# A fused retention and token-mixing kernel on one Trainium2 core: 64-row transposes, a transposed product for wq, other queues and a new order

## The chip, the cores and the metric

The kernel runs on one core of a Trainium2 chip. The core has a matrix engine (TensorE, PE in the profile, with its weight loads as PEld), three engines for elementwise work (VectorE or DVE, ScalarE or ACT, GpSimd or POOL), a queue engine that issues the transfers (SyncE or SP), and 16 DMA engines. Each engine works through its own instructions in the order of the program and waits for the others by semaphores. TensorE writes to PSUM, which has eight banks; VectorE and ScalarE read it, GpSimd does not.

The metric is the time of one execution on the device in microseconds. Lower is better.

## The reference, cut to what matters

```
# q, k, v: [4, 8, 768, 64] f32; w_q, w_k: [512, 64]; w_out: [512, 512]
gamma[h] = 1 - 2 ** (-5 - h)
for t in range(768):
    state = gamma * state + k[t] v[t]^T          # per batch and head, 64 x 64
    y[t]  = q[t] state / sqrt(64)
x  = y, heads side by side                       # [4, 768, 512]
wq = x @ w_q                                     # [4, 768, 64]
wk = x @ w_k
mixed = (wq wk^T / sqrt(64)) @ x                 # over the tokens of a batch
out   = relu(mixed) @ w_out                      # [4, 768, 512] f32
```

## The kernel before

The 768 tokens of a batch are cut into three pairs of chunks of 128 tokens; with four batches there are 12 pairs, numbered 0 to 11. The first half of the work on a pair is the retention in chunked form. The decay is put into v (factors `fv`) and into the result (factors `fy`), so that within a chunk the result is a masked product of scores with v, and between chunks a running state of 64 x 64 for each head is kept in PSUM bank 7. The second half is the mixer: wq and wk of the pair, then, once for each batch, z = wk^T x (`zm`), then for each pair mixed^T = z^T wq^T (`mx`), relu and the product with w_out (`pj`).

Nothing is scheduled by a compiler. A list of tokens, `ORDER`, is written out by hand and run through once; each token emits the instructions of one step. A token reads `name.pair.part:engine@bank`. `ck`, `cq` and `cv` cast the loaded k, q and v to bf16 (v with its factors); `trk` and `trq` transpose k and q on TensorE into PSUM, `ekT` and `eqT` copy them out; `sc` makes the scores of half the heads, `eat` masks them on VectorE; `st` adds to the state, `es` copies it out; `ia` and `in` are the products within a chunk and with the state; `ex` writes x. `xt` and `exT` transpose x; `wqk` makes wq and wk in one product; `ewq` copies wq out (twice side by side), `ew` copies wk; `tw` transposes wq and `ewt` copies it; `zm`, `ez`, `mx`, `r`, `pj` and `eo` follow. `W` and `WO` cast the weights. `fill` emits matmuls on zeros, whose results nobody reads.

A transpose of 128 rows by 128 columns is one TensorE instruction with a weight load; a pair has 8 each in `trk` (L344), `trq` (L359) and `xt` (L483), and 2 in `tw` (L523). The scores (L379) and the products with the state (L419) have 64 rows, and their two halves of heads lie in the upper and the lower 64 rows of the array and in different banks. The other line numbers that the text uses: L137 is a copy or cast on ScalarE, L138 one on VectorE or GpSimd, L292 the fills, L316 `cv`, L391 `eat`, L433 `st`, L453 `ia`, L467 `ex`, L497 `wqk`, L545 `zm`, L565 `mx`, L587 `pj`, L616 the stores, L156 the loads.

All transfers but the first go through the SP queue, in the order of a second list:

```
LOADS = """
q0 v0 k1 q1 v1 k2 q2 v2 k3 q3 v3 w k4 q4 v4 k5 q5 v5 o k6 q6 v6 k7 q7 v7 k8 q8 v8 k9 q9 v9 k10
q10 s0 v10 k11 s1 q11 s2 v11 s4 s3 s5 s6 s7 s8 s10 s11/0 s11/1 s9
""".split()
```

`k3` is the load of k of pair 3 (512 KB in pieces of 512 bytes), `w` and `o` are the weights, `s4` is the store of pair 4, and `s11/0` that of half a pair. There are 18 staging slots for k, q and v; a load waits until the cast of the load 18 places before it is done, and a store until both halves of its pair are copied out. The weights have staging of their own. Ten buffers hold results that wait for their store.

Of the kernel before, what the change touches and what calls it, by code (L numbers as in the profile page):

```python
# [9 lines left out]
FP32 = mybir.dt.float32  # L10
# [6 lines left out]
ck.0.1:V cq.0.0:A ck.0.0:P fill.20@6 trk.0@6 cq.0.1:V trq.0@0 cv.0.0:V ekT.0:A eqT.0:A st.0.0  # L17
ck.1.1:V ck.1.0:A cv.0.1:P sc.0.0@0 eat.0.0:V es.0.0:A sc.0.1@2 eat.0.1:V fill.1@6 trk.1@6
cq.1:A fill.3@0 trq.1@0 st.0.1 cv.1.0:P ia.0.1@2 ekT.1:A ck.2.0:A in.0.1@2 eqT.1:V ia.0.0@2
sc.1.0@0 es.0.1:A sc.1.1@4 cq.2:A ck.2.1:P st.1.0 ex.0:V trk.2@6 cv.1.1:P trq.2@2 eat.1.1:V  # L20
es.1.0:A eat.1.0:V eqT.2:A ekT.2:V ck.3.1:A ck.3.0:A xt.0@4 st.1.1 sc.2.0@2 cv.2.0:P cq.3:A
sc.2.1@0 exT.0:V es.1.1:V cv.2.1:P ia.1.0@4 cv.3.0:P in.1.0@4 eat.2.0:V in.1.1@4 ia.1.1@4
cv.3.1:P ck.4.1:P ex.1:V st.2.0 in.2.0@2 fill.1@6 trk.3@6 es.2.0:A cv.4.0:P cv.4.1:P fill.1@4
trq.3@4 ekT.3:A eat.2.1:V W:A ia.2.0@2 eqT.3:V ia.2.1@2 in.2.1@2 xt.1@6 sc.3.0@4 ex.2:V st.3.0
wqk.0@0 xt.2@1 exT.1:A wqk.1@6 es.3.0:A sc.3.1@2 eat.3.0:V ewq.0:A in.3.1@4 exT.2:V st.3.1
wqk.2@1 ew.0:A cq.4:A ia.3.0@4 eat.3.1:V ewq.1:A ewq.2:V ew.2:V ia.3.1@4 tw.1@2 ex.3:V cv.5.0:P
ew.1:A ck.4.0:A trq.4@6 trk.4@3 tw.0@1 ewt.1:V tw.2@0 es.3.1:A ck.5.1:A ekT.4:V eqT.4:V ck.5.0:A
ewt.2:A xt.3@4 st.4.0 cq.5:A fill.2@2 sc.4.0@2 trk.5@6 ewt.0:A exT.3:V ekT.5:V zm.0@4 trq.5@5
ez.0:A cv.5.1:P WO:P sc.4.1@0 es.4.0:A eat.4.0:V st.4.1 cq.6:P mx.0@2 eat.4.1:V eqT.5:A cv.6.0:P
es.4.1:A sc.5.1@4 sc.5.0@0 r.0:A wqk.3@6 st.5.0 eat.5.1:V in.4.0@2 mx.2@4 eat.5.0:V ewq.3:A  # L30
ia.4.1@2 in.4.1@2 es.5.0:V ck.6.1:A ck.6.0:A r.2:A cv.6.1:P ia.4.0@2 ew.3:V ia.5.1@0 in.5.0@0
ex.4:V in.5.1@0 ia.5.0@0 ex.5:V pj.0.0@6 trk.6@2 xt.4@3 trq.6@4 ekT.6:V pj.0.1@5 eo.0.0:A xt.5@6
eqT.6:V mx.1@0 exT.4:A exT.5:V ck.7.0:A sc.6.0@2 eat.6.0:V ck.7.1:P r.1:A st.6.0 cv.7.0:P tw.3@4
pj.2.0@6 cq.7:A wqk.4@0 es.6.0:V ew.4:V eo.2.0:A sc.6.1@2 wqk.5@1 trq.7@6 eat.6.1:V ewt.3:A
trk.7@4 ew.5:V ewq.4:A st.6.1 ewq.5:A ekT.7:V cv.7.1:P eqT.7:A pj.1.0@1 tw.4@6 es.6.1:V eo.0.1:V
ia.6.1@2 ck.8.1:A eo.1.0:A ia.6.0@2 in.6.1@2 cv.8.1:P sc.7.0@4 ewt.4:V cq.8:A st.7.0 zm.1@6
sc.7.1@0 ex.6:V trq.8@2 es.7.0:A eat.7.0:V cv.8.0:P ez.1:A xt.6@6 ck.8.0:A pj.1.1@3 exT.6:V
eat.7.1:V trk.8@4 pj.2.1@6 mx.4@0 eqT.8:A eo.1.1:A mx.3@2 st.7.1 r.4:V ekT.8:A sc.8.0@4 eo.2.1:A
ck.9.1:P wqk.6@6 es.7.1:A cq.9:P r.3:A st.8.0 ck.10.0:P ewq.6:A ia.7.1@0 ew.6:A ia.7.0@0
sc.8.1@2 in.7.0@0 es.8.0:A in.7.1@0 eat.8.0:V cq.10:P eat.8.1:V in.8.0@4 ck.9.0:A in.8.1@4  # L40
pj.4.0@6 eo.4.0:A ck.10.1:A ex.7:V cv.9.0:P ia.8.0@4 ia.8.1@4 pj.3.0@2 tw.5@6 cv.9.1:P trk.9@3
ex.8:V ewt.5:A trq.9@0 trq.10@6 eqT.9:V eqT.10:V ekT.9:A xt.8@4 sc.9.0@0 eat.9.0:V st.9.0
trk.10@3 eo.3.0:A ekT.10:V pj.4.1@6 exT.8:A ck.11.0:P sc.9.1@0 ck.11.1:A mx.5@4 es.9.0:V
eat.9.1:V xt.7@3 wqk.8@2 eo.4.1:A trk.11@6 ia.9.1@0 r.5:A exT.7:A cq.11:P ia.9.0@0 in.9.1@0
ewq.8:V cv.10.0:P ew.8:A sc.10.0@4 cv.10.1:P st.9.1 tw.6@3 ekT.11:V cv.11.0:P wqk.7@6 trq.11@2
ex.9:V ewt.6:A tw.8@3 eat.10.0:V ew.7:A es.9.1:A eqT.11:A ewq.7:A ewt.8:V pj.3.1@0 eo.3.1:V
xt.9@1 sc.11.0@2 sc.10.1@4 exT.9:A pj.5.1@6 pj.5.0@1 tw.7@0 st.10.0 eat.11.0:V eat.10.1:V
eo.5.0:V eo.5.1:A ewt.7:V zm.2@6 es.10.0:A ez.2:A st.10.1 es.10.1:V in.10.1@4 sc.11.1@2
cv.11.1:P in.10.0@4 mx.6@0 ia.10.1@4 eat.11.1:V r.6:A wqk.9@6 ia.10.0@4 st.11.0 mx.7@0 ex.10:V
r.7:A pj.6.0@2 eo.6.0:A es.11.0:V ewq.9:V ia.11.1@4 ew.9:A ia.11.0@4 in.11.0@4 in.11.1@4 mx.8@0  # L50
xt.10@6 pj.6.1@2 ex.11:V exT.10:A xt.11@3 r.8:A wqk.10@6 eo.6.1:V exT.11:V pj.7.1@4 ew.10:V
ewq.10:V eo.7.1:A wqk.11@3 ew.11:A tw.9@6 pj.7.0@2 ewq.11:A tw.10@3 ewt.10:V zm.3@4 ewt.9:A
pj.8.0@6 ez.3:V tw.11@3 eo.7.0:A eo.8.0:A mx.10@4 mx.9@0 ewt.11:V mx.11@2 pj.8.1@6 r.10:A
pj.10.1@4 r.11:V pj.10.0@5 eo.10.1:V pj.11.1@2 pj.11.0@4 eo.8.1:A eo.10.0:A r.9:V pj.9.0@6
eo.9.0:A pj.9.1@5 eo.11.0:V eo.9.1:A eo.11.1:V
# [14 lines left out]
def kernel(  # L70
# [15 lines left out]
    nc = tc.nc  # L86
# [24 lines left out]
    wstage_pool = pool("wstage", 1)  # L111
    const_pool = pool("const", 1)
    cast_pool = pool("cast", 3)
    qkt_pool = pool("qkt", 2)
# [4 lines left out]
    wqn_pool = pool("wqn", 3)  # L119
# [25 lines left out]
    wq_stage = wstage_pool.tile([128, NDM, DH], FP32, name="wq_stage")  # L145
    wk_stage = wstage_pool.tile([128, NDM, DH], FP32, name="wk_stage")
    wout_stage = wstage_pool.tile([128, NDM, DM], FP32, name="wout_stage")
# [14 lines left out]
    def load_token(token):  # L162
        if token == "w":
            nc.sync.dma_start(out=wq_stage, in_=moe_w_q.rearrange("(a p) h -> p a h", p=128))
            nc.sync.dma_start(out=wk_stage, in_=moe_w_k.rearrange("(a p) h -> p a h", p=128))
        elif token == "o":
            for a in range(NDM):
                nc.sync.dma_start(
                    out=wout_stage[:, a], in_=moe_w_out[128 * a : 128 * a + 128, :], max_dma_last_dim=512
                )  # L170
        else:
            load(token[0], int(token[1:]))
# [10 lines left out]
    def more_loads():  # L183
        while queue:
# [30 lines left out]
    ln_y = const_pool.tile([128, NP * 2, 2, HP], FP32, name="ln_y")  # L215
    for h in range(H):
        x, hp = divmod(h, HP)
        ln = math.log(1.0 - 2.0 ** (-5.0 - h))
        nc.vector.memset(ln_v[:, :, h, :], -ln)
        nc.vector.memset(ln_y.rearrange("p (cp x) c hp -> p cp x c hp", x=2)[:, :, x, :, hp], ln)  # L220
# [8 lines left out]
    ty = const_pool.tile([128, NP * 2, 2, HP], FP32, name="ty")  # L229
    ty_b = const_pool.tile([128, NP * 2, 2, HP], FP32, name="ty_b")  # L230
    for t, base in ((ty, 0), (ty_b, 1 - C)):
        for x in range(2):
            nc.gpsimd.iota(
                t.rearrange("p (cp x) c hp -> p cp x (c hp)", x=2)[:, :, x].rearrange(
                    "p cp (c hp) -> p cp c hp", c=2
                ),
                pattern=[[2 * C, NP], [C, 2], [0, HP]],
                base=base,
                channel_multiplier=2,
                allow_small_or_imprecise_dtypes=True,  # L240
            )
    nc.gpsimd.tensor_copy(out=ty[64:128], in_=ty_b[64:128])
    fv = const_pool.tile([128, NP, H, 2], FP32, name="fv")
    fy = const_pool.tile([128, NP * 2, 2, HP], FP32, name="fy")
# [4 lines left out]

    identity = const_pool.tile([128, 128], BF16, name="identity")  # L250
# [3 lines left out]
    cmask = const_pool.tile([128, 1, 2, G], BF16, name="cmask")  # L254
    cmask_b = const_pool.tile([128, 1, 2, G], BF16, name="cmask_b")

    def masks():

        for t, base in ((cmask, 0), (cmask_b, 127)):
# [39 lines left out]
    def ck(e, b, p, c):  # L299
# [366 lines left out]
```

## Time and profile before

| what | before |
|---|---|
| time, median of 3 runs | 102.17 us (101.83 to 104.67) |
| span of the profiled execution | 99.8 us |
| granted TensorE clock, mean | 0.955 |
| TensorE busy, weight loads busy | 86.5 us, 60.0 us |
| VectorE, ScalarE, GpSimd busy | 75.3, 72.5, 66.8 us |
| DMA: moved, mean rate | 26.68 MB, 267 GB/s |
| DMA: read and written in HBM | 20.19 MB, 6.29 MB |
| instructions | 3208 |

The profile is of one execution, and its span goes from the first to the last instruction of the program. The profiled execution's own device time is not given beside it; the span is 2.4 us shorter than the median of the timed runs, and what lies around it is taken from that difference. Matmuls are pipelined, and their ends are modelled, so that TensorE's busy time says less than the distance from one group's start to the next. A timeline row gives the start, the busy time, the engine, the line, the operation with what it writes and reads, the shape (rows * columns of the weights, then the output) and the number of instructions; in square brackets stands the idle time before it and what ended that.

### The profile page before, as it was taken

The page shows a single profiled execution, that of the slowest core. Times are in us where ns is not written, and L with a number is a line of the kernel's source. Part 1 is how long each engine was busy: PE and PEld are TensorE (multiplying, and loading weights), DVE is VectorE, ACT ScalarE, POOL GpSimd, SP SyncE. Part 2 cuts the span into 40 slices and gives each one's busy share as a digit, 9 for nine tenths or more (in the row PEclk, how much of TensorE's full clock was granted, in tenths as well). Part 3 has the DMA queues.
Part 4 walks back from the last instruction along what each step waited for, and adds up shares of the span by engine and source line. Part 5 has one row for each costly group of instructions (what it writes and reads, how often), then busy time and mean ns, then how long its engine had stood idle before and what let it go on. Part 6 is the DMA issues. An engine that isn't in the chain of part 4 may idle for free.

```text
span 99.8 us, 3208 instructions
## 1 busy us (share of the span) xinstructions
PE 86.5 (87%) x1319; PEld 60.0 (60%) x1332; DVE 75.3 (75%) x114; ACT 72.5 (73%) x123; POOL 66.8 (67%) x82
## 2 busy tenths in 40 slices
PE   4994669968999899989987999999899999999920
PEld 1344537857798666666865667768666776644400
DVE  3066972999999899967989678999969988227800
ACT  4126977199799996799899998999784567754130
POOL 6566589998969689769999999995699930000000
PEclk9999955699999999999999999999999999999995
DMA  1999999999999999999999999899967600762995
GB/s 22 283 348 347 347 347 349 285 253 276 323 298 295 327 290 322 270 312 336 338 343 346 323 300 305 255 317 341 290 204 217 204 13 7 210 210 69 317 290 167
DMA packets 53134, 26.68 MB, mean 267 GB/s; under 512 B 1920, under 2 KB 53120, under 8 KB 53120
## 3 DMA queue, kind: packets, MB, share of 16 engines
q1 hardware_dynamic: 52592, 26.22, 89.5%
q10 hardware_dynamic: 528, 0.26, 0.9%
q8 instruction: 10, 0.16, 0.6%
q14 instruction: 4, 0.03, 0.1%
HBM read 20.19 MB, written 6.29 MB: 265 GB/s over the span
## 4 chain that ended last, share of the span: by engine, by line
PE 41%; DVE 23%; DMA 14%; ACT 10%; issue 5%; SPq 1%; POOL 1%; ACTq 0%; DVEq 0%; POOLq 0%
PE banks L587 16%; DVE at_sb L391 11%; DMA q_st<-in_q_dram 7%; DMA v_st<-in_v_dram 6%; PE banks L453 4%; ACT ks L137 4%; DVE x_nat L467 4%; PE banks L483 3%; PE banks L379 3%; ACT o_st L137 3%; PE banks L497 2%; DVE vs L316 2%; PE banks L359 2%; PE banks L419 2%; PE banks L433 2%
## 5 line engine op out<-in xcount | busy, mean ns | idle before, releaser
L316 POOL TENSOR_TENSOR vs<-v_st,fv 64x512 bf16<-64x512 f32 x46 | 48.9, 1062 | 8.3 <-DMA v_st<-in_v_dram 3.7
L391 DVE TENSOR_TENSOR at_sb<-banks,cmask 128x1024 bf16<-128x1024 f32 x24 | 28.8, 1218 | 0.6 <-ACT s_sb L137 0.4
L587 PE MATMUL banks<-wout_sb,relu 128*128 128x512 bf16 x86 | 22.5, 379 | 0.8 <-ACT wqn L137 0.2
L137 ACT CAST ks<-k_st 64x512 bf16<-64x512 f32 x30 | 18.6, 619 | 1.8 <-DMA k_st<-in_k_dram 1.5
L467 DVE TENSOR_TENSOR x_nat<-banks,fy 128x1024 bf16<-128x1024 f32 x12 | 14.5, 1220 | 2.1 <-PE banks L453 1.1
L137 ACT COPY o_st<-banks 128x512 f32<-128x512 f32 x17 | 10.0, 589 | 6.6 <-PE banks L587 6.4
L587 PEld LDWEIGHTS <-relu 128*128 128x128 bf16 x96 | 8.5, 98 | 8.5 <-issue 0.8
L137 ACT CAST qs<-q_st 128x1024 bf16<-128x1024 f32 (+1 forms) x8 | 8.0, 996 | 3.7 <-DMA q_st<-in_q_dram 3.7
L292 PE MATMUL banks<-warm 128*128 128x512 bf16 x25 | 8.8, 507 | 2.1 <-DVE warm L211 1.3
L379 PE MATMUL banks<-qT,kT 64*128 64x128 bf16 x192 | 9.2, 225 | 1.4 <-DVE kT L138 0.9
L580 ACT ACTIVATE relu<-banks 128x1024 bf16<-128x1024 f32 x9 | 9.3, 1035 | 1.2 <-PE banks L565 1.2
L138 POOL CAST ks<-k_st 64x512 bf16<-64x512 f32 x14 | 8.9, 633 | 1.6 <-DMA k_st<-in_k_dram 1.0
L453 PE MATMUL banks<-vs,at_sb 128*128 128x64 bf16 x192 | 9.0, 197 | 0.3 <-DVE at_sb L391 0.2
L344 PE MATMUL banks<-identity,ks 128*128 128x128 bf16 x96 | 7.8, 224 | 1.0 <-ACT ks L137 0.6
L359 PE MATMUL banks<-identity,qs 128*128 128x128 bf16 x96 | 7.8, 227 | 1.0 <-ACT qs L137 0.5
L453 PEld LDWEIGHTS <-at_sb 128*128 128x128 bf16 x192 | 7.3, 100 | 1.8 <-DVE at_sb L391 0.5
L379 PEld LDWEIGHTS <-kT 64*128 64x128 bf16 x192 | 6.0, 98 | 3.7 <-issue 1.3
L433 PE MATMUL banks<-vs,ks 128*64 128x64 bf16 x160 | 6.5, 205 | 1.8 <-DVE vs L316 1.8
L359 PEld LDWEIGHTS <-qs 128*128 128x128 bf16 x96 | 6.3, 102 | 2.7 <-ACT qs L137 1.1
L483 PE MATMUL banks<-identity,x_nat 128*128 128x128 bf16 x96 | 7.4, 219 | 0.1
L344 PEld LDWEIGHTS <-ks 128*128 128x128 bf16 x96 | 6.1, 100 | 2.3 <-ACT ks L137 1.3
L497 PE MATMUL banks<-wqk_w,xT 128*128 128x128 bf16 x96 | 7.4, 219 | 0.1
(60 smaller groups left out, 123.2 us busy)
## 6 DMA issues: line engine op xcount, KB each, us to landing
q_st<-in_q_dram SPq DMA_DIRECT2D x12, 512.0 KB, 6.3
v_st<-in_v_dram SPq DMA_DIRECT2D x12, 512.0 KB, 6.5
k_st<-in_k_dram SPq DMA_DIRECT2D x11, 512.0 KB, 6.2
out_dram<-o_st SPq DMA_DIRECT2D x11, 512.0 KB, 3.3
wout_stage<-in_moe_w_out_dram SPq DMA_DIRECT2D x4, 256.0 KB, 5.3
out_dram<-o_st SPq DMA_DIRECT2D x2, 256.0 KB, 2.3
k_st<-in_k_dram ACTq DMA_DIRECT2D x1, 256.0 KB, 4.3
k_st<-in_k_dram SPq DMA_DIRECT2D x1, 256.0 KB, 4.0
```

What stands on the lines that cost most here:

```text
L137: return nc.scalar.copy(out=out, in_=in_)
L316: ENGINES[e].tensor_tensor(out=st["vs"][rows(j), c].rearrange("p hp x d -> p x hp d"), in0=st["v_st"][rows(c), :, :, j], in1=fv[rows(c), p ...
L344: nc.tensor.transpose(ps[:, hp, c], st["ks"][:, c, hp].rearrange("p x d -> p (x d)"), identity)
L359: nc.tensor.transpose(ps[:, hp, :, j, :], st["qs"][:, hp, j].rearrange("p x d -> p (x d)"), identity,)
L379: nc.tensor.matmul(out=ps[:, x, hi, c, :], lhsT=st["kT"][rows(x), hp, c, :], rhs=st["qT"][rows(x), hp, c, :], start=(hi == 0 and c == 0), ...
L391: ENGINES[e].tensor_tensor(out=st["at", half].rearrange("p x hi c t -> p (x hi c) t"), in0=st["at_ps", half].rearrange("p (n t) -> p n t", ...
L453: nc.tensor.matmul(out=y[:, x, c, hp, :], lhsT=st["at", half][:, x, hi, c, :], rhs=st["vs"][:, c, hp, x, :], start=first(p, x), stop=False ...
L467: nc.vector.tensor_tensor(out=st["x"].rearrange("p x c i n -> p (x c i n)").rearrange("p (m d) -> p m d", d=D), in0=st["y_ps"].rearrange(" ...
L483: nc.tensor.transpose(ps[:, a, c, :], st["x"][:, a // 2, c, a % 2, :], identity)
L497: nc.tensor.matmul(out=ps[:, c, :], lhsT=st["xT"][:, a, c, :], rhs=wqk_sb[:, a, :], start=(c == 0 and a == 0), stop=(a == NDM - 1), skip_g ...
L580: nc.scalar.activation(out=dst, in_=st["mx_ps"], func=ACT.Relu)
L587: nc.tensor.matmul(out=bank32(b), lhsT=st["relu"][:, a, j, :], rhs=wout_sb[:, a, :], start=(a == 0), stop=(a == NDM - 1),)
```

## The change

The names of the steps stay, and so does what is computed.

- `trk`, `trq` and `xt` emit 16 transposes of 64 rows in place of 8 of 128 rows. The upper and the lower 64 rows go to different banks; k and q of a pair share one pair of banks, each in a half of both. The copies (`ek`, `eq`, `exT`) read both half banks in runs of 64 elements, and kT and qT lie in one tile `kq`.
- `wqk` makes wk as before (8 matmuls, now of 64 columns) and wq already transposed and doubled (4 matmuls with w_q, which `W` now casts twice side by side, as weights, and 256 columns of x). `ewq` and `tw` are gone, and `ewt` copies from the product's bank in f32.
- `zm` comes in two parts: the first two pairs of a batch, then the third.
- The weights use the staging slots of k, q and v: `w` one and `o0` and `o1` one each, in other places of `LOADS`, and `WO` is two casts, one on VectorE and one on ScalarE in place of one on GpSimd.
- All stores stand behind the last load, in the order in which pairs are finished, those of pairs 9 to 11 in halves, in pieces of 2 KB; there are 11 result buffers.
- The bf16 tiles of k, q and v have 6 buffers for k, 4 for q and 6 for v in place of 3; the mask is made by a token of its own on GpSimd, and the factors for y are built in another layout and rearranged by three small GpSimd copies.
- `ORDER` is new throughout, with other engines for many copies and casts, and with 34 fills in place of 28.

The new file also has a second form of most steps, chosen by `TYPES`. All twelve entries of `TYPES` are "1", so that form emits nothing; the steps that run are those with a 1 in their names and the ones shown below. The diff, cut to its core:

```diff
 LOADS = """
-q0 v0 k1 q1 v1 k2 q2 v2 k3 q3 v3 w k4 q4 v4 k5 q5 v5 o k6 q6 v6 k7 q7 v7 k8 q8 v8 k9 q9 v9 k10
-q10 s0 v10 k11 s1 q11 s2 v11 s4 s3 s5 s6 s7 s8 s10 s11/0 s11/1 s9
+q0 v0 k1 q1 v1 k2 q2 w v2 k3 q3 v3 k4 q4 v4 o0 o1 k5 q5 v5 k6 q6 v6 k7 q7 v7 k8 q8 v8 k9 q9 v9 k10
+q10 v10 k11 q11 v11 s0 s1 s2 s3 s4 s5 s6 s7 s8 s9/0 s9/1 s10/0 s10/1 s11/0 s11/1
 """.split()
+TYPES = "111111111111"
-OBUFS = 10
+OBUFS = 11
+CASTS = dict(k=6, v=6, q=4)
+WBYTES = 512
+OBYTES = 2048
...
-            if token not in "wo":
-                n = len(staged)
-                if n >= STAGES and staged[n - STAGES] not in cast:
-                    return
-                staged.append(token)
+            n = len(staged)
+            if n >= STAGES and staged[n - STAGES] not in cast:
+                return
+            staged.append(token)
...
+    def half_banks(b, k):
+        return banks[:, b : b + 2, :].bitcast(BF16)[:, :, 512 * k : 512 * k + 512]
...
-    def trk(e, b, p):
-        ps = bank16(b).rearrange("p (hp c t) -> p hp c t", hp=HP, c=2)
-        for c in range(2):
-            for hp in range(HP):
-                nc.tensor.transpose(
-                    ps[:, hp, c], st["ks"][:, c, hp].rearrange("p x d -> p (x d)"), identity
-                )
+    def trk1(e, b, p):
+        ps = half_banks(b, 0).rearrange("p j (hp c g) -> p j hp c g", hp=HP, c=2)
+        for hp in range(HP):
+            for c in range(2):
+                for j in range(2):
+                    nc.tensor.transpose(
+                        ps[:, j, hp, c],
+                        st["ks"][rows(j), c, hp].rearrange("p x d -> p (x d)"),
+                        identity[rows(j), rows(j)],
+                    )
...
+    def ek1(e, b, p):
+        copy(e, st["kT"].rearrange("p hp c (j g) -> p j (hp c) g", j=2), st["ktr_ps"])
...
     def xt(e, b, p):
-                nc.tensor.transpose(ps[:, a, c, :], st["x"][:, a // 2, c, a % 2, :], identity)
+                for i in range(2):
+                    x_sb = ... st["x"][rows(i), a // 2, c]
+                    nc.tensor.transpose(ps[:, i, a, c], x_sb[:, a % 2, :], identity[rows(i), rows(i)])
...
     def wqk(e, b, p):
+        st["wk_ps"] = bank32(b)[:, 0:128].rearrange("p (c n) -> p c n", c=2)
+        st["wq_ps"] = bank32(b)[:, 256:512]
         for c in range(2):
             for a in range(NDM):
-                nc.tensor.matmul(out=ps[:, c, :], lhsT=st["xT"][:, a, c, :], rhs=wqk_sb[:, a, :], ...)
+                nc.tensor.matmul(out=st["wk_ps"][:, c, :], lhsT=st["xT"][:, a, c, :],
+                                 rhs=wqk_sb[:, a, 2 * DH :], ...)
+        for a in range(NDM):
+            nc.tensor.matmul(out=st["wq_ps"], lhsT=wqk_sb[:, a, 0 : 2 * DH],
+                             rhs=st["xT"][:, a].rearrange("p c t -> p (c t)"), ...)
-    def ewq(e, b, p): ...
-    def tw(e, b, p): ...
     def ewt(e, b, p):
-            st["tw_ps"].rearrange("p (c j g) -> p c j g", c=2, j=2),
+            st["wq_ps"].rearrange("p (c j g) -> p c j g", c=2, j=2),
-    def zm(e, b, bt):
-        for cp in range(NP):
+    def zm(e, b, bt, part):
+        for cp in (0, 1) if part == 0 else (2,):
...
-        nc.sync.dma_start(out=dst, in_=src, max_dma_last_dim=512)
+        nc.sync.dma_start(out=dst, in_=src, max_dma_last_dim=OBYTES)
```

The parts of the new `ORDER` that the text comes back to, the start, the stretch of pairs 5 and 6, and the end:

```
mask:P cq.0.1:A cv.0.0:P ck.0.1:V cq.0.0:V ck.0.0:A fill.15@6 trk.0@0 ck.1.0:A ck.1.1:A cv.0.1:P
cv.1.1:P cq.1:A trq.0@0 ck.2.1:P eq.0:V ek.0:V fill.6@6 st.0.0 sc.0.1@0 sc.0.0@2 cv.1.0:P ck.2.0:A
...
pj.1.0@6 eat.4.0:V eo.1.0:V xt.3@4 st.4.0 trq.5@2 trk.5@2 cv.8.1:P exT.3:A es.4.0:V ia.4.1@0
eq.5:V st.4.1 ia.4.0@0 ek.5:V in.4.0@0 in.4.1@0 ex.4:V es.4.1:A sc.5.1@2 sc.5.0@4 st.5.0 cv.9.1:P
eat.5.0:V xt.4@0 wqk.3@6 eat.5.1:V ck.6.0:A cv.9.0:P cq.6:A es.5.0:A trk.6@4 exT.4:A in.5.1@0
...
wqk.10@6 xt.11@3 exT.11:V ew.10:V pj.8.0@0 wqk.11@3 ew.11:V eo.8.0:V ewt.10:A zm.3.0@6 ewt.11:V
zm.3.1@6 ez.3:A mx.9@3 r.9:A mx.11@5 mx.10@0 pj.8.1@2 pj.9.0@3 pj.9.1@4 r.10:V pj.10.0@0 r.11:V
pj.10.1@1 eo.8.1:A eo.10.0:V eo.10.1:V eo.9.0:A pj.11.0@5 eo.11.0:V pj.11.1@0 eo.9.1:A eo.11.1:V
```

More of the change, by code (lines that the diff above doesn't have):

```diff
@@ new lines, in cross @@
+    def cross(e, b, p):
+        st = pairs[p]
+        y = y_of(p, b)
+        new = [first(p, 0) if carried(p, 0, 1) else False, first(p, 1)]
+        for hp in range(HP):
+            for j in range(2):
+                for c in range(2):
+                    x = 1 - c
+                    if not carried(p, c, x):
+                        continue
+                    s_sb = st["s", 0] if c == 1 else pairs[p - 1]["s", 1]
+                    nc.tensor.matmul(
+                        out=y[rows(j), c, x, hp, :],
+                        lhsT=st["kq"][rows(x), c, 1, hp, j],
+                        rhs=s_sb[rows(x), hp, :],
+                        start=new[c] and hp == 0,
+                        stop=False,
+                        skip_group_check=True,
+                    )
@@ new lines, in state @@
+    def state(e, b, p, c):
+        cp = p % NP
+        st = pairs[p]
+        for hp in range(HP):
+            for j in range(2):
+                for x in range(2):
+                    nc.tensor.matmul(
+                        out=state_ps[rows(x), hp, :],
+                        lhsT=st["ks"][rows(c), hp, j, x, :],
+                        rhs=st["vs"][rows(c), hp, j, x, :],
+                        start=(cp == 0 and c == 0 and hp == 0 and j == 0),
+                        stop=(cp == NP - 1 and hp == HP - 1 and j == 1),
+                        skip_group_check=True,
+                    )
@@ new lines, in es, with ia @@
+    def es(e, b, p, c):
+        pairs[p]["s", c] = s_pool.tile([128, HP, D], BF16, name="s_sb")
+        copy(e, pairs[p]["s", c], state_ps)
+    def ia(e, b, p, half):
+        st = pairs[p]
+        y = y_of(p, b)
+        for hi in range(2):
+            hp = 2 * half + hi
+            for x in range(2):
+                for j in range(2):
+                    for c in range(2):
+                        nc.tensor.matmul(
+                            out=y[:, c, x, hp, :],
+                            lhsT=st["at", half][rows(c), x, hi, j, :],
+                            rhs=st["vs"][rows(c), hp, j, x, :],
+                            start=first(p, c),
+                            stop=False,
+                            skip_group_check=True,
+                        )
```

459 lines of the change are left out of this document (307 added, 152 removed).

## The prediction

> **What bounds the kernel now.** I read the page's shares first, then the chain that ended last, then TensorE's timeline, then the groups.
>
> ```profile
> span 99.8 us, 3208 instructions
> PE 86.5 (87%) x1319; PEld 60.0 (60%) x1332; DVE 75.3 (75%) x114; ACT 72.5 (73%) x123; POOL 66.8 (67%) x82
> PEclk9999955699999999999999999999999999999995
> q1 hardware_dynamic: 52592, 26.22, 89.5%
> ```
>
> No engine is full over the span, but the DMA queue is close (89.5%), and a load of 512 KB passes in about 1.5 us (347 GB/s in the page's best slices). TensorE's clock is halved only near 12 to 20 us. The chain, in order of time:
>
> ```profile
> 63.38 7.33 DMA q_st<-in_q_dram
> ...
> 70.82 1.05 POOL qs L138
> ...
> 71.92 0.62 PE banks L359 x8
> ...
> 89.21 6.17 PE banks L587 x28
> 95.38 0.02 issue
> 95.40 0.59 ACT o_st L137
> ```
>
> The last q load (q11) lands at 70.7, its cast ends at 71.9, and from there to 95.4 the chain is TensorE alone. So the loads hold the kernel until about 72 us and TensorE's own queue after that. One pair earlier in the middle shows the same hand-over, in ScalarE's and TensorE's timelines:
>
> ```profile
> 40.42 2.50 ACT L137 CAST ks<-k_st 64x512 bf16<-64x512 f32 x4 [0.67 <-DMA k_st<-in_k_dram]
> 42.98 0.62 PE L344 MATMUL banks<-identity,ks 128*128 128x128 bf16 x8 [0.45 <-ACT ks L137]
> ```
>
> k6 lands at 40.4, ScalarE casts it in two tokens, and trk.6 starts at 42.98. I use that start as the anchor.
>
> **What a TensorE step costs.** Matmuls overlap, so busy time is no price; the distance from one group's start to the next is.
>
> ```profile
> 68.95 0.61 PE L344 MATMUL banks<-identity,ks 128*128 128x128 bf16 x8
> 69.39 0.63 PE L453 MATMUL banks<-vs,at_sb 128*128 128x64 bf16 x16
> 69.96 0.29 PE L419 MATMUL banks<-s_sb,qT 64*128 64x64 bf16 x8
> 70.08 0.39 PE L379 MATMUL banks<-qT,kT 64*128 64x128 bf16 x8
> 70.40 0.32 PE L433 MATMUL banks<-vs,ks 128*64 128x64 bf16 x8
> 70.70 0.27 PE L523 MATMUL banks<-identity,wqn 128*128 128x128 bf16 x2
> 70.81 0.61 PE L497 MATMUL banks<-wqk_w,xT 128*128 128x128 bf16 x8
> ```
>
> Eight 128-row transposes take 0.44 (56 ns each), 8 matmuls of 64 rows and 64 columns only 0.12 (14.4 ns: the two row halves run side by side), 16 of 128 rows and 64 columns about 0.46 (29 ns). A change of tile shape adds 0.1: at 62.02 the same 16 of L453 are followed 0.46 later by L587 of the same shape, here 0.57 later by a 64-row form. Other steps by the same reading: a score half (8 of L379) 0.21, a state step 0.14, a whole zm 0.62, an mx 0.22, a fill 0.216, a pj 0.86.
>
> **The change, part by part.** (1) Transposes: trk, trq and xt become 16 of 64 rows by 64 columns. No transpose of this size is in the trace. Nearest row in shape is L419, 16 x 14.4 = 0.23 against 0.45. The bounds: 28.8 ns each if the two halves do not overlap (0.46, no gain) and 56 ns if a transpose costs what L344's does (0.90). I take 14.4, because L419 has exactly these weights, columns and two target banks. (2) wqk: 8 of 64 columns (0.23) and 4 of 256 (half of a pj's 216 ns, about 0.11 each, 0.44), 0.67 against 0.45; tw goes (0.11). Per pair 3 x 0.22 + 0.11 - 0.22 = 0.55, over 12 pairs 6.6 us less. (3) Against it: changes of tile shape along the queue go from 84 to 95 (1.0 us) and fills from 28 to 34 (1.3). TensorE's queue sums to 78.4 us before and 74.2 after.
>
> The page "TensorEngine Tiling (Array Packing)" of the Trainium skill, Key Properties, states that a change of tiling mode drains TensorE, a rule against splitting transposes between full-height steps. The trace agrees, at 0.1 us a change; without it this queue would be worth another 1.0 us.
>
> (4) ewq goes: 8 x 0.39 on ScalarE and 4 x 0.42 on VectorE. ewt now reads f32 from PSUM: on VectorE 0.42 like the wqn copy instead of 0.29, on ScalarE 0.38 as before. WO leaves GpSimd (1.89) for one half on ScalarE (about 1.05, its q cast of that size) and one on VectorE (0.7 to 1.1; 0.44 for half a q gives about 0.75). The copies of the transposes read two half banks in runs of 64; wqT's copy already writes such runs at 0.29 for 256, the rate of 0.69 for 1024, so I add nothing; the upper end is f32 speed, 0.5 more for each of 36. k's and q's copy of one pair share banks and exclude each other, up to 0.7 late where they are on two engines (pairs 6 and 11). From pair 2's first eat to ex.11 VectorE now holds 20 eat and 11 ex at the 1.14 between neighbours (35.3), 21 copies of transposes and outputs at 0.60 (12.6), three cq and half of WO at 0.65 (2.6), five ewt and three es at 0.33 (2.6), three ew at 0.2 (0.6): 53.7. Before, it was busy 54.0 of the 60.5 us between the same places (22.4 to 82.9). VectorE is not relieved. (5) GpSimd keeps 23 of 24 cv (2.1 each) and gains the mask's five instructions (1.3) and three small copies, which lie in the 8.2 us before v0 lands; uncovered, 1.3. More cast buffers (6, 6, 4 for 3) can only spare GpSimd its 2.1 us of waits on TensorE, off the path: nothing. (6) Lead-in: ScalarE casts q0's half, then k0's (2 x 0.62), so trk.0 comes at 8.5, not 7.66. Behind it TensorE had idled 1.77 before L433; that hides it, and without it 0.8 us is lost. z in two parts is the same 12 matmuls.
>
> (7) The SP queue: s0, s1 and s2 no longer stand before v10, q11 and v11. Three stores of 1.5 us leave, so v11, before issued at 66.95 and landed 7.5 later, lands near 70, and q11 near 67.7. The weights of wout now pass before k5, not after v5: k5, q5, v5 come 3.0 later, k6 as before. Weights in stage slots cannot hold up SP: a load waits for the cast 18 tokens back, and SP reaches k8 at 43.6, some 20 us after v2's cast; if casts fell behind that far, each late us would be one on the loads. More TensorE instructions (about 640 with weight loads) are fetched by the same DMA engines; the page has 10 such fetches of 0.16 MB together, two more are under 1 us of one engine. All stores queue behind v11: 12 x 1.5 = 18.1, so DMA can end at 88 at the earliest, just under TensorE. Descriptors of 2 KB: stores already reach 345 GB/s within a transfer, so nothing.
>
> **The sum.** From trk.6 on TensorE's queue holds 49.2 before (23 pj, 20 transpose groups, 41 changes) and 44.8 after (21 pj, 19 groups of 0.23, 48 changes). Check on before: 43.0 + 49.2 = 92.2 against 95.4 seen, so 3.2 us of waits. After: k6 lands unchanged, TensorE has only 29.4 us of queue ahead of trk.6 and 35 us for it, so 43.0 + 44.8 + 3.2 = 91.0. The tail: before, 95.4 to 99.8 held a 0.59 copy, a 512 KB store (2.9) and 0.9 of closing, 4.4; after, a VectorE copy of 0.69, a 256 KB store (2.3) and 0.9: 3.9. Span 94.9, that is 4.9 less than 99.8. The measured median is 102.17, 2.4 over the profiled span; with that 2.4 kept, **97.3**. With no waits TensorE (87.8) and the stores (88) end together, 94.2; with twice the waits 100.5. Its own range is 94.2 to 100.5.
>
> **Rivals.**
> A, the gain ends in VectorE. It has the same work and idled 6.5 of 60.5 us. If the late k5, q5 and v5 push it by 3.0 (eat.5 cannot start before their copies, and everything on VectorE queues behind) and its idle time stays, ex.11 ends at 22.4 + 53.7 + 6.5 + 3.0 = 85.6; behind it TensorE has 10.2. Span 85.6 + 10.2 + 3.9 = 99.7, time 102.1. For: VectorE was busy without a gap from 20 to 25 and from 35 to 40. Against: between 43 and 59 it waited six times by 0.3 to 0.9, mostly for TensorE, which is what the change shortens.
> B, the change does not do what it says: the halves of a transpose do not overlap, 28.8 ns each. Then 19 groups cost 0.23 more from trk.6 on, 4.4 us: 101.7. For: no row shows a 64-row transpose. Against: L419 and L379 overlap.
> C, slower: a 64-row transpose costs the 56 ns of L344, by a fixed price of each. Its place is the queue behind trk.6, its price 19 x 0.67 = 12.7, so 110; it decides from 28 ns on, where the gain is used up. Against: the distance follows the columns in every full-clock row from 64 to 512.
> D, small: a halved clock as at 12 to 20 us, in the bound stretch; 8 us of it costs 4. Against: the clock stayed 1.00 with TensorE over 80% busy.
>
> **How the numbers follow.** A measurement of this kernel tells 2% from no change, so the borders are 100.1 and 104.2. Chances: forecast 0.64, A 0.13, B 0.08, C 0.06, D or several of them 0.09. Faster: 0.60 from the forecast, 0.08 from the rest (A with less idle, D early). Same: 0.18, from A, B and D. Slower: 0.14, from C, D and pile-ups of A and B. Holding the time 8 times in 10 needs the forecast's range and the upper rivals A and B, so 93.6 to 102.6; C is left out above.
>
> **What would show it.** Right: groups of 16 transposes 0.23 to 0.3 from start to next start; q11 landing near 67.7 and v11 near 70; TensorE's last matmul near 91; the first store after v11's issue; VectorE's busy time unchanged or up by a few us. Wrong: transposes at 28 ns or more; ex.11 ending after 83 with VectorE waiting for DMA or casts; SP waiting ahead of loads; or a halved clock after 20 us.

## The result and the profile after

The changed kernel takes 98.5 us (median of 4 runs, 97.57 to 98.9), against 102.08 (101.83 to 104.67, 4 runs) for the kernel before: a ratio of 0.9639 [0.957, 0.9707]. A second set of runs of the same two kernels, told below as the run `again`, gave 0.9741 [0.964, 0.9842]. Ratios compare undisturbed executions only, so that they stand above the ratio of plain medians where the kernel before had many disturbed ones; the profiles of `t64_in_turn` and `dve_less` below are of disturbed executions and are read for the order of events, not for the total. The profiled execution has a span of 95.9 us and a time of its own of 97.57, that is 1.7 over the span.

The page of the changed kernel, lines that answer to those shown of before:

```profile
span 95.9 us, 3812 instructions
PE 81.0 (84%) x1634; PEld 52.8 (55%) x1650; DVE 78.7 (82%) x114; ACT 68.4 (71%) x113; POOL 65.9 (69%) x82
PEclk9999999999759999999999999999999999999999
```

TensorE lost 5.5 us of busy time although it has 315 matmul instructions more; VectorE gained 3.4 and is now nearly as busy. The end of the chain of waits, in order of time:

```profile
68.91 0.62 ACT ks L136
69.55 0.38 ACT s_sb L136
...
83.88 0.29 DVE wk_n L137
84.17 0.60 DVE o_st L137
84.76 0.34 DVE wqT L137
85.15 0.83 PE banks L809 x12
86.14 6.00 PE banks L831 x27
92.17 0.69 DVE o_st L137
```

Before, the chain was TensorE alone from 71.92 on. Now, behind 62 us, it steps off TensorE twice, at 69 to a ScalarE cast and the copy of the state behind it, and at 84 to three VectorE copies in a row, for the last of which the last `mx` (L809) waits. The steps themselves, in TensorE's timeline (L605 is `trq`, L585 `trk`, L627 `sc`, L809 `mx`):

```profile
50.01 0.40 PE L627 MATMUL banks<-kq 64*128 64x128 bf16 x8
50.24 0.40 PE L605 MATMUL banks<-identity,qs 64*128 64x64 bf16 x16
50.47 0.40 PE L585 MATMUL banks<-identity,ks 64*128 64x64 bf16 x16
50.71 0.38 PE L809 MATMUL banks<-wqT,z_sb 64*128 64x256 bf16 x4
```

Start to start, 16 transposes of 64 rows take 0.23 us, 14.4 ns each.

A caution about the profile of before. Its span of 99.8 holds a stretch of halved clock at 12 to 20 us, and the same instructions ran faster in a later profile, the run `b_stores_last`, whose transfers are issued in the same order up to 56 us and whose `ORDER` is the same. Its page and its timeline around pair 2's `trk` (L344; L292 are the fills):

```profile
span 98.1 us, 3211 instructions
PEclk9999999999999999999999999999999999999995
```

```profile
13.10 0.81 PE L292 MATMUL banks<-warm 128*128 128x512 bf16 x3 [0.23 <-DVE at_sb L391]
...
16.29 0.62 PE L344 MATMUL banks<-identity,ks 128*128 128x128 bf16 x8
```

In the profile of before the same three fills took 1.44, and pair 2's `trk` started at 18.68: 2.4 later. It was still 1.6 late at pair 6's `trk` (42.98 against 41.37) and 1.7 at the end of TensorE's queue (95.38 against 93.67). Traces whose clock was whole up to the last 3 us on both sides, `b_stores_last` with 98.1 and `again` with 95.5, are 2.6 apart, which agrees with the 0.9741 above. But the profiled execution does not stand out in the first set: with 1.7 around its span it took some 101.5 us, and all four times of that set are longer. In the later sets the compared executions of the kernel before took 99.3 to 101.2, with mean clocks from 0.95 to 1.00 and no difference by clock. So the kernel before took some 1.5 to 2 us longer throughout the first set, and why is not shown.

### The profile page after: what moved, and what is told of

Same layout as the page of the kernel before. It is cut to its first block, busy times and chain, and to the rows that moved or that the text cites. A ratio compares the mean times of both kernels' runs of the same rounds, so it can differ in the third digit from the quotient of the medians.

```text
span 95.9 us, 3812 instructions
## 1 busy us (share of the span) xinstructions
PE 81.0 (84%) x1634; PEld 52.8 (55%) x1650; DVE 78.7 (82%) x114; ACT 68.4 (71%) x113; POOL 65.9 (69%) x82
## 4 chain that ended last, share of the span: by engine, by line
PE 37%; DMA 21%; SPq 17%; POOL 9%; ACT 5%; DVE 4%; issue 3%; DVEq 0%; ACTq 0%
PE banks L831 16%; SPq L151 14%; DMA v_st<-in_v_dram 14%; POOL vs L556 7%; DMA q_st<-in_q_dram 7%; PE banks L758 3%; PE banks L627 3%; PE banks L698 3%; SPq L166 2%; PE banks L809 2%; ACT relu L824 2%; PE banks L749 2%; ACT ks L136 2%; PE banks L678 2%; PE banks L730 2%
## 5 line engine op out<-in xcount | busy, mean ns | idle before, releaser
L556 POOL TENSOR_TENSOR vs<-v_st,fv 64x512 bf16<-64x512 f32 x46 | 49.4, 1074 | 6.7 <-DMA v_st<-in_v_dram 3.8
L712 DVE TENSOR_TENSOR x_nat<-banks,fy 128x1024 bf16<-128x1024 f32 x12 | 14.6, 1220 | 1.1 <-PE banks L698 0.9
L137 DVE COPY kq<-banks 128x1024 bf16<-128x1024 bf16 x14 | 9.1, 683 | 2.4 <-PE banks L605 2.3
L136 ACT COPY kq<-banks 128x1024 bf16<-128x1024 bf16 x10 | 9.7, 1014 | 1.3 <-PE banks L585 0.7
L136 ACT COPY o_st<-banks 128x512 f32<-128x512 f32 x14 | 8.2, 589 | 1.8 <-PE banks L831 1.8
L627 PE MATMUL banks<-kq 64*128 64x128 bf16 x192 | 8.7, 225 | 0.9 <-DVE at_sb L639 0.3
L627 PEld LDWEIGHTS <-kq 64*128 64x128 bf16 x192 | 6.3, 98 | 3.8 <-issue 2.6
L585 PE MATMUL banks<-identity,ks 64*128 64x64 bf16 x192 | 5.0, 190 | 3.2 <-ACT ks L136 1.9
L136 ACT CAST qs<-q_st 128x1024 bf16<-128x1024 f32 (+1 forms) x5 | 4.8, 959 | 3.9 <-DMA q_st<-in_q_dram 3.8
L758 PE MATMUL banks<-xT,wqk_w 128*128 128x256 bf16 x48 | 7.2, 273 | 0.0
L136 ACT CAST s_sb<-banks 128x256 bf16<-128x256 f32 x15 | 5.7, 378 | 1.9 <-PE banks L678 1.8
L137 DVE COPY o_st<-banks 128x512 f32<-128x512 f32 x10 | 6.7, 682 | 0.3 <-PE banks L831 0.2
```

What stands on the lines that cost most here:

```text
L136: return nc.scalar.copy(out=out, in_=in_)
L137: return ENGINES[e].tensor_copy(out=out, in_=in_)
L556: ENGINES[e].tensor_tensor(out=st["vs"][rows(j), c].rearrange("p hp x d -> p x hp d"), in0=st["v_st"][rows(c), :, :, j], in1=fv[rows(c), p ...
L627: nc.tensor.matmul(out=ps[:, x, hi, c, :], lhsT=st["kT"][rows(x), hp, c, :], rhs=st["qT"][rows(x), hp, c, :], start=(hi == 0 and c == 0), ...
L712: nc.vector.tensor_tensor(out=st["x"].rearrange("p x c i n -> p (x c i n)").rearrange("p (m d) -> p m d", d=D), in0=st["y_ps"].rearrange(" ...
L758: nc.tensor.matmul(out=st["wq_ps"], lhsT=wqk_sb[:, a, 0 : 2 * DH], rhs=st["xT"][:, a].rearrange("p c t -> p (c t)"), start=False, stop=(a ...
```

## The experiments

Two theories were to be told apart. By the first, the prediction's, TensorE's queue behind pair 6's `trk` is the bound, and each us on it counts in full. By the second, rival A, VectorE is the bound, and the shorter transposes are worth little. On the changed kernel, the gain was also to be shared out over the parts. Each run compares with the kernel before on its own chip. The first four shared one chip, the next four another, the last four the second one again.

**`t128`: transposes of 128 rows back, all else as after.**

```diff
-                for j in range(2):
-                    nc.tensor.transpose(ps[:, j, hp, c], st["ks"][rows(j), c, hp]..., identity[rows(j), rows(j)])
+                nc.tensor.transpose(ps[:, hp, c], st["ks"][:, c, hp]..., identity)   # trq and xt likewise
```

> The changed kernel with transposes of 128 rows again (k in the first bank of the pair, q in the second, x in the first), all else as changed. Theory (TensorE's queue behind trk.6 is the bound, and the 64-row transposes pay for the gain): 19 groups of 0.45 instead of 0.23 behind trk.6 (+4.2 us) and 52 changes of tile shape instead of 48 (+0.4): about 103 us, group distance 0.45. Rival (the earlier loads and the new order pay for the gain, TensorE has room): within 1 us of the changed kernel's 98.5.

Measured 99.88, ratio 0.9916 [0.9868, 0.9965]. A group of 8 now takes 0.45, which puts 19 x 0.22 = 4.2 us back on the queue behind trk.6. Against the two runs below that keep the short transposes on the same chip (0.9738 and 0.9733) it costs 1.8% or 1.8 us, good to about 1: neither the whole 4.2 of the theory nor the less than 1 of the rival. Windows of `t128` and of after from pair 6's `trk` to TensorE's end show why (columns: the stretch, its length, then busy time and instructions of TensorE, weight loads, VectorE, ScalarE, GpSimd, the granted clock, the share of DMA, GB/s):

```profile
43.00:94.30 51.30, 50.48 (x782) 33.09 (x780) 43.23 (x54) 36.73 (x63) 31.21 (x32) 1.00 0.76 248
```

```profile
43.00:92.00 49.00, 45.73 (x924) 29.86 (x927) 43.07 (x54) 36.86 (x63) 32.21 (x33) 1.00 0.82 267
```

By its busy time TensorE idles 0.8 us of the stretch with long transposes and 3.3 with short ones. About half of what the transposes give up turns into waits of TensorE for the engines that feed it, whose work is the same in both.

**`t64_in_turn`: 64-row transposes, but the 8 of one half before the 8 of the other.** Do the halves overlap only when they alternate?

```diff
-        for hp in range(HP):
-            for c in range(2):
-                for j in range(2):
+        for j in range(2):
+            for hp in range(HP):
+                for c in range(2):   # trq and xt likewise
```

> The same 64-row transposes as in the changed kernel, but all 8 of one half of the rows first and then all 8 of the other, so that neighbours share the same rows of the array. If the gain comes from two halves running side by side: 28 ns each, 0.45 a group, 19 groups x 0.22 = 4.2 us behind trk.6, about 102.7 us. If each 64-row transpose is simply short (14.5 ns whatever stands beside it): 98.5 us, as the changed kernel.

Measured 99.43, ratio 0.9853 [0.9782, 0.9924]: about 1.2 us slower than with alternating halves. The step is about 23 ns in place of 14.4, 0.14 more a group and at most 2.7 on the queue; it costs less than half of that too. Neither of the expected steps came, 28 ns or 14.5. The trace shows why it is in between: of two neighbouring groups the starts mix.

```profile
53.13 0.44 PE L605 MATMUL banks<-identity,qs 64*128 64x64 bf16 x13
53.39 0.20 PE L585 MATMUL banks<-identity,ks 64*128 64x64 bf16 x1
53.41 0.19 PE L605 MATMUL banks<-identity,qs 64*128 64x64 bf16 x1
53.43 0.19 PE L585 MATMUL banks<-identity,ks 64*128 64x64 bf16 x1
```

The first transposes of k (upper rows) start before the last ones of q (lower rows) that stand ahead of them in the program. Each half of the rows works through its own instructions; alternating them in the program only keeps both halves fed.

**`stores_early` and `pieces_512`: the stores at their old places; the stores in pieces of 512 bytes.**

```diff
-q10 v10 k11 q11 v11 s0 s1 s2 s3 s4 ...
+q10 s0 v10 k11 s1 q11 s2 v11 s3 s4 ...        # stores_early
```

```diff
-OBYTES = 2048
+OBYTES = 512                                  # pieces_512
```

> The changed kernel with s0 before v10, s1 before q11 and s2 before v11 again, the other stores last. Theory: the loads of q11 and v11 come about 2.5 and 3.7 us later (stores of 2 KB pieces take 1.2 us), but TensorE has that much queued ahead of trk.11 and ia.11: 0 to 1 us longer, 98.5 to 99.5. Rival (the order of the stores is where the gain comes from): 3 us or more, 101.5 and up.

> The changed kernel with stores in pieces of 512 bytes. Theory: stores move at 347 instead of 404 GB/s, which only the last halves at the end can show, 0.1 us each: 98.5 to 98.8, same. Rival (the stores at the end set the time): all twelve take 18.1 us instead of 15.5, 2 us or more longer, 100.5.

Measured 98.04, ratio 0.9738 [0.9579, 0.9898], and 98.45, ratio 0.9733 [0.9515, 0.9951]. Neither can be told from the changed kernel (0.9639 and 0.9741). To within the 1.6 to 2.2% of these intervals, neither the end of the loads nor the rate of the stores is a bound here.

**`again`, `pe_more`, `dve_more`, `act_more`: the changed kernel itself, and with work added to one engine.** `pe_more` has 18 fills (3.9 us) in front of `pj` steps behind trk.6; `dve_more` multiplies an unused tile on VectorE ahead of six `ex`; `act_more` copies it on ScalarE ahead of six `r`.

```diff
+ fill.3                         # pe_more: ahead of pj.2.0, 3.0, 4.0, 5.0, 6.0, 7.0, in their banks
+ more:V                         # dve_more: ahead of ex.6 to ex.11
+ more:A                         # act_more: ahead of r.3 to r.8
+    def more(e):
+        if e == "A": nc.scalar.copy(out=extra, in_=extra)
+        else: nc.vector.tensor_tensor(out=extra, in0=extra, in1=extra, op=ALU.mult)
```

> The changed kernel itself, beside the next three: 98 to 98.5 us.

> The changed kernel with three fills (0.216 us each) ahead of one pj of each of pairs 2 to 7, 3.9 us more on TensorE alone behind trk.6, spread over the stretch. Theory as predicted (TensorE is the bound from trk.6 on): 3.9 us longer than the changed kernel beside it. Theory after the 128-row run (TensorE has about 2.3 us of waits there that extra work fills first): 1.5 to 2 us longer. Rival A (VectorE is the bound): under 1 us.

> The changed kernel with one more VectorE instruction (128 x 512 f32 times itself, about 0.6 us) ahead of each ex of pairs 6 to 11, 3.6 us more on VectorE alone. If TensorE alone is the bound: under 1 us longer. Rival A (VectorE is the bound): 3 us or more. If the two share the bound: 1 to 2.5 us.

> The changed kernel with one more ScalarE copy (128 x 512 f32, about 0.6 us) ahead of each relu of pairs 3 to 8, 3.6 us more on ScalarE alone. Theory: ScalarE has the room (68.4 us busy of 95.9), under 1 us longer. Rival (ScalarE's relus stand on the way to pj): 2 us or more.

| run | added | median us | ratio to before | cost against `again`, per us added |
|---|---|---|---|---|
| `again` | nothing | 98.47 | 0.9741 [0.964, 0.9842] | |
| `pe_more` | 3.9 us TensorE | 100.59 | 0.9987 [0.9925, 1.0049] | 2.5, 0.6 |
| `dve_more` | 6.5 us VectorE | 101.95 | 1.0119 [1.0044, 1.0195] | 3.8, 0.6 |
| `act_more` | 3.7 us ScalarE | 99.93 | 0.9919 [0.9869, 0.997] | 1.8, 0.5 |

The cost is the difference of the ratios, with 1% taken as 1.0 us, since the kernel before takes about 100 us in the executions compared here; the interval of `again` alone, 1.0 either way, makes the price of one us good to about 0.2 to 0.3. Neither theory holds: a bound on one engine would give 1 for it and 0 for the others. Not all came as expected. `pe_more` fell between the 3.9 of the prediction and the 1.5 to 2 expected after `t128`. ScalarE does not have the room that was expected (under 1 us). And `dve_more` alone, with 3.8 us for six instructions, is what rival A expected (3 or more); what speaks against A are `pe_more`, for which A allowed under 1 us, and `dve_less` below. `dve_more` does not load VectorE alone either: between 43 and 95 us GpSimd is busy 1.6 us more (33.84 for 32.21). VectorE's addition is larger than was planned because its six instructions did not all take 0.6 (the last section has the reason); the trace's line for the tile, with the shortest, the median and the longest in ns:

```profile
L882 DVE TENSOR_TENSOR extra<-extra x6: 677/1048/1402, 53.8 to 84.3; 128x512 f32<-128x512 f32 x6
```

**`dve_less`: from pair 6 on `eat` masks only half of the scores**, so that part of the computation is left out and VectorE has 5.8 us less between 43 and 95 (38.0 busy for 43.8).

```diff
+        n = 4 if p >= 6 else 8
-            in0=st["at_ps", half].rearrange("p (n t) -> p n t", t=C),
+            in0=st["at_ps", half].rearrange("p (n t) -> p n t", t=C)[:, 0:n],
```

> The changed kernel with eat masking only half of the scores for pairs 6 to 11 (the other half of at_sb keeps what an earlier pair left, so half of these pairs' products within a chunk are left out of the computation in effect); TensorE's instructions are the same. VectorE gets 12 x about 0.5 = 6 us less. If VectorE shares the bound at 0.55: 3 us less, 95.3. If TensorE alone is the bound: under 1 us less, 97.7. If VectorE alone is: TensorE's 43.0 + 44.8 stops it near 94.5.

Measured 98.57, ratio 0.9799 [0.9696, 0.9901]: no faster than the changed kernel, to within some 1.4 us. Taking 5.8 us from VectorE did not gain the 3 us that a bound shared at 0.55 would give; its groups show where the time went:

```profile
L717 DVE TENSOR_TENSOR x_nat<-banks,fy 128x1024 bf16<-128x1024 f32 x12 | 14.6, 1220 | 3.2 <-PE banks L703 2.9 <-PE banks L669 0.2
...
L137 DVE COPY kq<-banks 128x1024 bf16<-128x1024 bf16 x14 | 9.1, 687 | 4.0 <-PE banks L605 3.2 <-PE banks L585 0.6 <-ACT kq L136 0.2
```

VectorE idles 3.2 and 4.0 us ahead of these two steps, for 1.1 and 2.4 in the changed kernel, and it waits for TensorE (`ia` and `trq`), as TensorE waits for VectorE and ScalarE in the changed kernel. The granted clock was 0.97 between 43 and 95 us in this execution, so that some of this can come from the clock. Its chain of waits runs over ScalarE from 61 to 72 us. So the engines are coupled through the order of the tokens: added work on one is felt in part, and of removed work part (TensorE) or all (VectorE, within the error) is lost in the next wait. That the order does this is argued from these waits and not shown; the one other order that was tried gained nothing.

**`order_2`: an attempt at a better order.** TensorE's gaps at 48.3, 70 and 85.2 wait for a q cast on VectorE, for a k cast on ScalarE and for VectorE's last copies, so `cq.7`, `ck.11.1` and `ewt.11` were moved back or ahead. The expectation speaks of five tokens and of q casts that go to ScalarE; in the kernel that ran, three tokens moved and all three q casts are still on VectorE, so that its sum for the casts does not apply.

```diff
- cq.7:V xt.5@0 exT.5:V          + xt.5@0 exT.5:V cq.7:V
- ck.11.1:A zm.2.0@3 ... ez.2:A  + zm.2.0@3 ... ez.2:A ck.11.1:A
- ewt.11:V behind zm.3.0         + ewt.11:V behind ew.11:V
```

> The changed kernel with five tokens moved: the casts cq.4, cq.7 and cq.9 go from VectorE (1.0 to 1.4 us each there) to ScalarE (1.05), cq.7 behind exT.5; ck.11.1 stands behind ez.2 on ScalarE, so that es.9.0 no longer waits for it; ewt.11 stands ahead of eo.8.0 on VectorE, so that mx.9, which uses its bank, starts 0.6 earlier. If VectorE is the fullest and an added us costs 0.55 on it and 0.4 on ScalarE: 3.6 x 0.55 - 3.2 x 0.4 = 0.7 and 0.5 at the end, 97.3 us beside a changed kernel of 98.5. If TensorE's queue is the bound: only the 0.5 at the end, 98.

Measured 99.49, ratio 0.9848 [0.9719, 0.9976], no gain and not the 97.3 or 98 expected; its profiled span is 95.9, that of the changed kernel. The gap at 85 did not close: `mx` starts at 85.18 and by the chain it follows an output copy on VectorE instead.

```profile
84.57 0.61 DVE o_st L139
85.18 0.82 PE banks L811 x12
```

No version faster than the changed kernel was found.

**`b_stores_last` and `b_wq_product`: one part alone, put into the kernel before.** In the first, s0, s1 and s2 stand behind v11. In the second, wq is made transposed by its own product; `ewq` and `tw` are gone, and `ewt` stands at the place of `ewq`.

```diff
-q10 s0 v10 k11 s1 q11 s2 v11 s4 s3 ...
+q10 v10 k11 q11 v11 s0 s1 s2 s4 s3 ...         # b_stores_last
```

```diff
-                nc.tensor.matmul(out=ps[:, c, :], lhsT=st["xT"][:, a, c, :], rhs=wqk_sb[:, a, :], ...)
+                nc.tensor.matmul(out=st["wk_ps"][:, c, :], lhsT=st["xT"][:, a, c, :], rhs=wqk_sb[:, a, 2 * DH :], ...)
+        for a in range(NDM):
+            nc.tensor.matmul(out=st["wq_ps"], lhsT=wqk_sb[:, a, 0 : 2 * DH], rhs=st["xT"][:, a]..., ...)
```

> The kernel before with s0, s1 and s2 behind v11 and nothing else changed. q11 lands 3 us earlier, v11 4.5 us. If the loads hold the kernel until trq.11 (71.9 + 23.0 of queue): up to 3 us less, 99. Theory (the queue behind trk.6 is full anyway, and only its waits can shrink): 0 to 1 us less, 101 to 102.

> The kernel before with wq made transposed by its product, ewq and tw left out and ewt in the place of ewq; nothing else changed. TensorE: 12 x (0.22 - 0.11) = 1.3 more and up to 9 changes of tile shape fewer behind trk.6; ScalarE 3.1 and VectorE 1.7 less and one hand-over less on the way to mx. Theory as in the sum (TensorE counts): 0 to 1 us longer. Rival (the copies count): 1 us less or more.

Measured 100.22, ratio 1.0018 [0.9973, 1.0063]: the order of loads and stores is worth nothing in the old kernel either, although its profile's chain ran through the last q load. And 101.89, ratio 1.0204 [1.0133, 1.0276]: in the old order the product for wq costs 2%, more than the 0 to 1 us of the theory, and the rival, a gain, is out. It lengthens TensorE's queue by 0.22 a pair and takes away 0.11, 1.3 us in all, and the relief of ScalarE and VectorE, where `ewq` was, did not pay for it. The product is no gain by itself; why it costs more than 1.3 us was not traced.

## Why the prediction was right, step by step

- **The price of a 64-row transpose** was the main choice, and it was right: 14.4 ns, 13.8 to 14.9 in 31 of the 36 groups (two of the others lie in the stretch of halved clock, three hold a longer step), so that rivals B (28.8) and C (56) fall at once. `wqk` comes out at 8 x 29 ns + 4 x 109 ns = 0.67 as priced, a change of shape at 0.1. That a change of tiling mode drains TensorE, as the page "TensorEngine Tiling (Array Packing)" of the Trainium skill has it under Key Properties, agrees with that 0.1 again and is far too small to speak against the change.
- **The anchor**: trk.6 was put at 43.0 and started at 42.76, but not for the reason given. The working let it wait for k6's load and cast, with time to spare on TensorE. In the changed kernel k6 lands at 39.6 and its casts end by 41.6, and trk.6 starts 1.2 later, without idle time behind pair 3's `wqk`. That stands behind pair 4's `xt` (L730), which waits for VectorE: `ex` (L712) of that pair ran from 40.35 to 41.58.

```profile
41.63 0.41 PE L730 MATMUL banks<-identity,x_nat 64*128 64x64 bf16 x16 [0.41 <-DVE x_nat L712]
41.97 0.41 PE L749 MATMUL banks<-wqk_w,xT 128*128 128x64 bf16 x8
42.21 0.60 PE L758 MATMUL banks<-xT,wqk_w 128*128 128x256 bf16 x4
42.76 0.41 PE L585 MATMUL banks<-identity,ks 64*128 64x64 bf16 x16
```

  So the number was luck, twice: another wait took the place of the one named, and the anchor came from a trace that ran 1.6 late. Against `b_stores_last` (41.37) trk.6 is 1.4 us later in the changed kernel. k6 also lands 1.1 later there (39.6 for 38.5), though the same loads stand ahead of it; why was not tried. The sum counts the two `pj` that the new order moves ahead of trk.6 (2 x 0.86) as a gain behind it; with trk.6 that much later most of it is not there.
- **The step that failed: "waits 3.2 kept".** From trk.6 to TensorE's last matmul 49.4 us passed (42.76 to 92.14, predicted 43.0 to 91.0). With the queue at the 44.8 of the sum, the waits are 4.6 and not 3.2 (busy time, which counts overlapping ends, leaves the 3.3 shown above). They are no constant that can be added: over the same stretch `t128` has 51.9 (42.46 to 94.31) for a queue of 49.0, so 2.9 of waits. A us taken from TensorE's queue gave back some 0.4 as waits in that comparison, and on the clock of whole runs more than half. The working has this term as a carried-over remainder and prices its doubling only in the range, which is where the result fell.
- **VectorE's work** was put at 53.7 between pair 2's first `eat` and `ex.11`. It is 56.75 of 59.2:

```profile
22.40:81.60 59.20, 53.58 (x1260) 37.75 (x1271) 56.75 (x67) 50.61 (x86) 50.36 (x52) 0.97 0.96 297
```

  The terms that were most too small are the casts from staging:

```profile
L137 DVE CAST qs<-q_st 128x1024 bf16<-128x1024 f32 x3 | 3.8, 1265 | 0.4 <-DMA q_st<-in_q_dram 0.4
...
L137 DVE CAST wout_sb<-o_st 128x1024 bf16<-128x1024 f32 x1 | 1.0, 1005 | 0.2 <-DMA o_st<-in_moe_w_out_dram 0.2
```

  1.27 each and 1.0 for the 0.65 of the sum, about 2 of the 3 us: they wait for GpSimd (last section). The rest was not traced to single terms. The second q cast shows directly what it delays. It waits 0.35 for q7 and then holds up pair 5's copy `xT`, and TensorE's `wqk` (L749) waits 0.40 for that:

```profile
46.55 1.12 DVE L137 CAST qs<-q_st 128x1024 bf16<-128x1024 f32 x1 [0.35 <-DMA q_st<-in_q_dram]
47.59 0.68 DVE L137 COPY xT<-banks 128x1024 bf16<-128x1024 bf16 x1
```

```profile
48.33 0.41 PE L749 MATMUL banks<-wqk_w,xT 128*128 128x64 bf16 x8 [0.40 <-DVE xT L137]
```

- **Rival A** had this much right: VectorE is not relieved and leaves 2.4 us idle where 6.5 were. But k5, q5 and v5 came 3.0 to 3.5 us later than before without moving `ex.11` back, which ended at 81.6 and not at 85.6, and `dve_less` shows that VectorE alone is not the bound. VectorE is also what TensorE waited for ahead of trk.6. **D**: the granted clock fell only from about 25 to 29 us and was 1.00 from there to TensorE's end.
- **Loads and stores**: q11 landed at 66.6 and v11 at 68.1 (67.7 and 70 predicted), and the stores follow v11's issue:

```profile
61.46 1.60 SPq L151 DMA_DIRECT2D v_st<-in_v_dram  x1
63.16 3.40 SPq L860 DMA_DIRECT2D out_dram<-o_st  x3
```

  That they are off the path was assumed for the end of the queue; `stores_early` and `b_stores_last` show it for the last loads as well.
- **The tail** was 3.7 (92.2 to 95.9) for 3.9. **What lies around the span** is 1.7 us in each execution that has both figures, and not 2.4: the 2.4 set the span of a single execution against the median of others. The span was 1.0 above the 94.9 of the sum and this term 0.7 too large, so that the two errors nearly cancel in the predicted 97.3 against 97.57 for that execution, which is luck again. Of the gain, 4.9 us were forecast; 3.6 were measured in the first set and 2.6 in the second, where the forecast is nearly twice too large.

Where the gain comes from, some 2.6 us by the traces of `b_stores_last` and `again` and by the ratio of `again` (3.6 by the first, smaller set of runs): 1.8, good to about 1, are the 64-row transposes, by `t128` and its neighbours. That leaves some 0.8, no larger than its error. The two traces add up as follows: trk.6 comes 1.5 later (42.84 in `again`), the stretch to TensorE's end is 3.35 shorter (48.95 for 52.3), and the tail 0.7 (98.1 - 93.67 = 4.4 against 95.5 - 91.80 = 3.7), 2.6 in all; of the stretch 2.4 to 2.9 are gone again in `t128` (51.85). The shorter tail is the last store, which is half the size. What the new order gives by itself (two `pj` now stand ahead of the last stretch) was not isolated: no run has the old parts in the new order without the wq product, so the remainder is read from the traces and not shown.

## What to carry to other kernels

Work taken from one engine in a kernel of in-order queues that are all 70 to 85% busy need not be worth its time: here a us of TensorE work was worth 0.4 to 0.6, added or removed, 5.8 us off VectorE gained nothing measurable, and the remainder of waits had to be priced anew and not carried over. Price a new instruction by the row that has its shape and its pattern of row halves; a VectorE step between SBUF tiles needs the wait for GpSimd's instruction added. Before an anchor is taken from one trace, look whether its clock was whole up to there, and walk the new order to see which wait will end last there.

## What the runs showed of the hardware that was not expected

- **The VectorE casts and multiplications from SBUF to SBUF waited until GpSimd's current instruction was done, and GpSimd's next one took longer.** The q cast shown above started at 46.55 and took 1.12; GpSimd's `cv` beside it and the one behind:

```profile
46.08 1.04 POOL L556 TENSOR_TENSOR vs<-v_st,fv 64x512 bf16<-64x512 f32 x1
```

```profile
47.18 1.40 POOL L556 TENSOR_TENSOR vs<-v_st,fv 64x512 bf16<-64x512 f32 x1
```

  The first `cv` ends at 47.12, that is 0.57 into the cast, and the cast ends 0.55 later. The other two q casts (1.25 and 1.42) and the half of WO (1.00) end 0.55 behind the end of a `cv` as well, at 28.55, 60.13 and 33.57. The next `cv` lasts 1.40 in place of 1.04: it begins at 47.18, while the cast runs on to 47.67. A q cast that began only 0.10 before the end of a `cv`, at 46.57 in `again`, took 0.69, near the 0.65 of the working. In `dve_more` five of the six added multiplications fit with the same 0.55 (0.93 to 1.40), and the sixth, at 84.28 when GpSimd had finished, took 0.68. Copies that read PSUM kept their 0.68 beside a working GpSimd. The page "SBUF — State Buffer" of the Trainium skill, in its section on the two separate sides, describes this: a port pair that VectorE and GpSimd share, held by one of them for a whole instruction. The trace agrees, with the numbers above. The prediction priced these casts without that wait, and this is about 2 of the 3 us by which VectorE's work was too small.
- **Stores in 2 KB pieces moved faster.** In the slices where whole stores pass alone, the page of after (2 KB pieces, 67 to 74 us) has 385 to 404 GB/s, that of `pieces_512` (70 to 80 us) 343 to 346:

```profile
GB/s 9 273 347 347 347 347 318 282 340 340 265 319 258 317 302 301 318 336 313 273 344 340 329 318 274 331 329 359 404 398 385 60 229 0 196 23 38 404 321 119
```

```profile
GB/s 24 287 346 347 347 346 318 244 339 311 257 270 254 289 335 341 263 306 305 243 243 269 322 268 285 308 311 336 252 343 346 345 343 174 174 50 43 347 345 129
```

  The prediction had costed this at nothing. It is off the path here, and `pieces_512` takes the same time.
- **The two row halves of TensorE ran through these transposes independently**, across groups of different lines: 23 ns a transpose when the halves come in turn, 14.4 when they alternate, 0.14 us a group.
